# Two more chunks of a shared value quarter held in the lower half of a PSUM bank, with one bank for the weighted sums meanwhile

## The chip, the cores and the metric

The kernel runs on one core of a Trainium2 chip, in one launch. The metric is the time of the execution on the device in microseconds (us). Lower is better.

## What is computed

Eight batch rows, one token each, go through two identical layers. A layer is an attention step over a cache, added to its input, and then a small MLP mixer, added again. Both layers read the same weights and the same caches.

```python
B, Sq, D = 8, 1, 448
Hq, Hkv, Sk, Dh = 16, 8, 4096, 256
...
q = (x @ wq).reshape(B, Sq, Hq, Dh)            # transposed to B, Hq, Sq, Dh
scores = einsum("bhqd,bhkd->bhqk", q, k) * (Dh ** -0.5)
p = softmax(scores)
o = einsum("bhqk,bhkd->bhqd", p, v)            # back to B, Sq, Hq * Dh
return o @ wo
...
x = x + A(layernorm(x)); x = x + mixer_mlp(layernorm(x))     # layer 0
x = x + A(layernorm(x)); x = x + mixer_mlp(layernorm(x))     # layer 1
```

For each row and each of the 8 key-value heads there are 2 MB of keys and 2 MB of values (4096 x 256, bf16). Everything is needed once for layer 0 and, since the queries of layer 1 depend on the result of layer 0, once more for layer 1.

## The kernel before, in words

**Tiles and slots.** A head's 2 MB lie as 128 partitions x 32 positions x 256 values. They are loaded in quarters: a quarter is 8 chunks of 256 values on every partition, 4 KB per partition, 512 KB in all. SBUF has 30 slots for quarters (`QUARTERS`). A load of several neighbouring quarters can go out as one DMA; `next_kv` in the planner chooses slot and size, and `issue_kv` (L653 is the line of the DMA itself) writes the instruction.

**What is kept between the layers.** Some quarters of a row stay in their slots from layer 0 to layer 1: the keys of heads 3 to 6, the first quarter of the keys of head 7, the values of head 7, and quarters 1 to 3 of the values of head 6 (`KEPT_K`, `KEPT_V`). Two further quarters of the keys of head 7 wait as transposes in the four transpose banks of PSUM, and one more in `kh` and in the upper halves of the two banks `psP`. The first quarter of the values of head 6 (`PART_V`) is not kept whole. A part of it, `PART` = 512 of the 2048 values per partition (two chunks), is copied by ScalarE (ACT) into columns 256 to 511 of bank `psR` (L1318), after the first quarter's weighted sum in layer 0. In layer 1 the load of that quarter leaves out these values (`skip`), and ACT copies them back into the slot (L1277) when the rest has landed.

**A head's two halves of work.** `front(layer, b, h)` transposes the keys on TensorE (PE; L1544 into `psT`), evacuates them on VectorE (DVE) and ACT (L1473, L1474), forms the scores (L1156, or L1438 by rows) and the exponentials (L1246). `back(layer, b, h)` loads the values, forms the weighted sums in one of the two banks `psP`, quarter by quarter, copies the bank out (L1332 to L1338), turns it on PE into the same bank (L1345), reduces it on DVE (L1349, L1352), and projects it with `wo` (L1373, or L1093 for the last heads of a layer). The weighted sum has a wide form (L1289, whole bank) and a narrow one (L1296, lower half) that is used while the upper halves of `psP` hold keys (`upper`). The bank alternates with the count of backs:

```python
par = g % 2
ps, bk = psP[par], f"P{par}"
```

**The crossing.** For a row, heads 0 to 2 and then 3 to 7 pass layer 0. The MLP of layer 0, the queries of layer 1 and layer 1 follow, which begins with heads 6 and 7. Between head 7 of layer 0 and head 6 of layer 1 stand the backs of heads 0, 1 and 2 of the next row, whose values are loaded one quarter at a time. I call the stretch from head 6 of layer 0 to head 6 of layer 1 a crossing; there are eight, one per row, the first around 114 to 148 us, the third around 377 to 405, the sixth around 764 to 790. In the last crossing there is no next row, and backs of layer 1 of the row before stand in its place. Most slots hold kept quarters in a crossing, so the loads pass through the few others.

**The order of the work.** All operations are listed with their dependencies and priorities, and `schedule` lays them out with planned durations, engine by engine. The result is a fixed order for each engine, with semaphores. DMAs are issued by SP in order; an issue waits until the last reader of its slot is done. Where PE would stand idle in the plan, the planner puts in matmuls on an identity (`filler`, L1753), to hold the planned load of PE above a mark, and only into a bank that no operation has open (`bank_ev`).

Of the kernel before, what the change touches and what calls it, by code (L numbers as in the profile page):

```python
# [53 lines left out]
YC = 0  # L54
ST = 504
STR = 244
PART = 512
Q1 = 176
ROWS = True
SHORT = 0.1  # L60
# [2 lines left out]


class Op:
    __slots__ = ("dma_n", "eng", "emit", "dur", "deps", "prio", "idx", "name", "lat", "sem", "val",
                 "pos", "vc", "signal", "end", "nsucc", "succ", "raw", "dma", "tbank", "unit", "frees", "hot", "quiet")

    def __init__(self, eng, emit, dur, name, prio):
# [25 lines left out]
class Plan:  # L95
# [12 lines left out]
    def __init__(self):  # L108
        self.ops = []
        self.writer = {}  # L110
        self.readers = {}
        self.bank = {}
        self.filler = None
        self.issue_kv = None
        self.tenant = [None] * QUARTERS
        self.free_at = [0.0] * QUARTERS

    def op(self, eng, emit, dur, name, rd=(), wr=(), banks=(), prio=None, dma=None):
        o = Op(eng, emit, dur, name, len(self.ops) if prio is None else prio)
        o.idx = len(self.ops)  # L120
        o.dma = dma
        for k in rd:
            w = self.writer.get(k)
            if w is not None:
                o.deps[w] = True
        for k in wr:
            w = self.writer.get(k)
            if w is not None and w not in o.deps:
                o.deps[w] = False
            for r in self.readers.get(k, ()):  # L130
                if r is not o and r not in o.deps:
                    o.deps[r] = False
        for b in banks:
            for e, a in self.bank.get(b, {}).items():
                if a is not o and a not in o.deps:
                    o.deps[a] = False
        for k in rd:
            self.readers.setdefault(k, []).append(o)
        for k in wr:
            self.writer[k] = o  # L140
            self.readers[k] = []
        for b in banks:
            d = self.bank.setdefault(b, {})
            if eng == "pe":
                d["pe"] = o
            else:
                d[eng] = o
        self.ops.append(o)
        return o
# [15 lines left out]
    def schedule(self):  # L165
# [78 lines left out]
        while n < len(self.ops):  # L244
# [99 lines left out]
            quiet = quiet or o.quiet  # L344
            if o.tbank is not None:
                for x in o.tbank if isinstance(o.tbank, list) else [o.tbank]:
                    bank_ev[x] = True if e == "pe" else o
            o.pos = len(order[e])
            order[e].append(o)
            n += 1  # L350
# [131 lines left out]
def bass_interleave_layers__gqa_block_cached__mixer_s_mlp__decode_kernel(  # L482
# [125 lines left out]
    def slot_ap(x, a, n):  # L608

        return kv[:, x.slot * 2048 + a:x.slot * 2048 + a + n]  # L610
# [645 lines left out]
    def back(layer, b, h):  # L1256
# [5 lines left out]
        g = backs[0]  # L1262
        backs[0] += 1
        no = g % NO
        par = g % 2
        ps, bk = psP[par], f"P{par}"
        wide_pv = not upper[0]
        hi = len(plan.ops) - 10 ** 5
# [1 line left out]
        most = MOST if (layer == 0 and b and h in free_heads) else MOST2 if h == l2_heads[1] and layer else 4  # L1270
        if (layer, b, h) == (1, B - 1, free_heads[-1]):
            most = 1
        part = h == PART_V and layer
        assert not part or fresh_v == [0]
        vs.update(load(A_v_cache, b, h, fresh_v, keep_v, most, PART if part else 0))
        if part:
            plan.op("act", lambda a: a.copy(slot_ap(vs[0], 0, PART).bitcast(f32), psR[:, 2 * P:2 * P + PART // 2]), 0.4,  # L1277
                    "part", rd=["part", ("s", vs[0], 0)], wr=[("s", vs[0], 2)], banks=["R"], prio=hi)
        first = 4 * CH + len(plan.ops) if layer == 0 and b and h in free_heads else None
        turned = (layer, b) == (1, B - 1) and h in TURNED  # L1280
        for u in range(4):

            def pv(t, u=u, q=vs[u]):
                last = None
                for g in range(4 if wide_pv else 0):
                    k = 8 * g + 4 * (u // 2) + 2 * (u % 2) if in_rows else 8 * u + 2 * g
                    v = (slot_ap(q, 0, 2048).rearrange("p (a s x) -> p a s x", a=2, s=4)[:, :, g, :] if in_rows else
                         slot_ap(q, 512 * g, 512))
                    last = t.matmul(ps[32 * g:32 * g + 4, :], pT[nr][:, k:k + 2, :].rearrange("p k j -> p (k j)"),  # L1289
                                    v, start=(u == 0), stop=(u == 3), skip_group_check=True,  # L1290
                                    tile_position=(0, 32 * g))
                for s in range(0 if wide_pv else 8):
                    i = 8 * u + s
                    g4 = 32 * (i % 4)
                    k = 8 * (s % 4) + 4 * (u // 2) + 2 * (u % 2) + s // 4 if in_rows else i
                    last = t.matmul(ps[g4:g4 + 2, PV0:PV0 + DH], pT[nr][:, k, :],  # L1296
                                    slot_ap(q, s * 256, 256), start=(i < 4), stop=(i >= 28),
                                    skip_group_check=True, tile_position=(0, g4))
                return last

            def pv_turned(t, u=u, q=vs[u]):
                last = None
                for s in range(8):
                    k = 8 * (s % 4) + 4 * (u // 2) + 2 * (u % 2) + s // 4
                    for c in range(2):
                        last = t.matmul(ps[:, PV1 + 2 * c:PV1 + 2 * c + 2], slot_ap(q, s * 256, 256)[:, c:DH:2],
                                        pT[nr][:, k, :], start=(u == 0 and s == 0), stop=(u == 3 and s == 7),
                                        skip_group_check=True)
                return last
            fn, d = (pv_turned, (0.45, 0.47, 320, 16)) if turned else (pv, (0.25, 0.46, 512, 4 if wide_pv else 8))  # L1310
            o = plan.op("pe", fn, d, "pv",
                    rd=[("pT", nr, 0), ("pT", nr, 1), ("s", vs[u], 0), ("s", vs[u], 1),
                        "pz"] + [("s", vs[u], 2)] * bool(part and u == 0) + [("acc", 1) if u > 1 else ("o2", 1 - par)] * ((layer, b, h) == (1, B - 1, free_heads[-1]) and u > 0),
                    wr=[("pv", par, x) for x in range(u, 4)], banks=[bk], prio=first)
            if u == 0:
                o.tbank = bk
            if h == PART_V and not layer and u == 0:
                o = plan.op("act", lambda a: a.copy(psR[:, 2 * P:2 * P + PART // 2],  # L1318
                                                    slot_ap(vs[0], 0, PART).bitcast(f32)), 0.4, "part",
                            rd=[("s", vs[0], 0), ("pv", par, 0)], wr=["part"], banks=["R"], prio=hi)  # L1320
            if u not in keep_v:
                o.frees = [vs[u]]

# [94 lines left out]
    tcount = [0]  # L1418
    held_banks = set()
    upper = [False]  # L1420
    by_rows = {}

    def next_bank():
# [63 lines left out]
    def half_piece(x, pc):  # L1487

        if pc == 0:
            bank = tcount[0] % NT
            while tcount[0] % NT in held_banks:
                tcount[0] += 1
            bank = tcount[0] % NT
            tcount[0] += 1

            def tr(t):
                last = None
                for s in range(4):  # L1500
                    last = t.transpose(psT[bank][:, s * P:(s + 1) * P],
                                       slot_ap(x, s * 256, 256).bitcast(f32), ident_f[:, :])
                return last
            plan.op("pe", tr, (0.44, 0.86, 1024, 4), "tr", rd=[("s", x, 0), "ident_f"],
                    wr=[("psT", bank)], banks=[("T", bank)]).tbank = bank

            def ev(e):
                if e is nc.vector:
                    return e.tensor_copy(kh[:, :].bitcast(f32), psT[bank][:, :])
                return e.copy(kh[:, :].bitcast(f32), psT[bank][:, :])  # L1510
            plan.op("ev", ev, {"dve": 0.71, "act": 0.6}, "ev", rd=[("psT", bank)], wr=["kh", ("khb", 0), ("khb", 1)],
                    banks=[("T", bank)]).tbank = bank
            return
        upper[0] = True
        for i in range(2):
            def tr(t, i=i):
                last = None
                for s in range(2):
                    last = t.transpose(psP[i][:, DH + s * P:DH + (s + 1) * P],
                                       slot_ap(x, (4 + 2 * i + s) * 256, 256).bitcast(f32), ident_f[:, :])  # L1520
                return last
            plan.op("pe", tr, (0.25, 0.45, 512, 2), "tr", rd=[("s", x, 1), "ident_f"],
                    wr=[("ph", i)], banks=[f"P{i}"]).tbank = f"P{i}"
        for i in range(2):
            evac_half(i, lambda i=i: slot_ap(x, (4 + 2 * i) * 256, 512).bitcast(f32), ("s", x, 1, i))
# [287 lines left out]
```

## Time and profile before

| | |
|---|---|
| median of 3 runs | 1071.9 us (1071.61 to 1074.43) |
| profiled execution | 1069.21 us |
| its span, first to last instruction | 1067.4 us |
| PE busy | 944.8 us (89%) |
| DVE busy | 600.4 us (56%) |
| ACT busy | 337.4 us (32%) |
| main DMA queue | 432.79 MB, 98.6% of 16 engines' span |
| mean granted PE clock | 0.975 |
| copies into `psR` (L1318) | 8, median 0.376 us |
| copies out of `psR` (L1277) | 8, median 0.358 us |

Durations come from the one profiled execution, and the times from separate runs. Busy times are a union over an engine's instructions. The granted clock is the share of full speed that TensorE's throttle let through. The share of the DMA engines is the time that their packets took; it can come out slightly above 1 in a short stretch, since a packet is counted where it starts.

### The profile page before, as it was taken

What the parts mean: (1) busy time and instruction counts of PE and PEld (TensorE: products, weight loads), DVE (VectorE), ACT (ScalarE), POOL (GpSimd) and SP (SyncE); (2) the same over time, 40 slices, a digit from 0 to 9 for tenths busy, and PEclk for the clock granted to TensorE, in tenths of its full rate; (3) what the DMA queues carried; (4) which work ended last, traced back from release to release, by engine and by line L of the source; (5) the groups of instructions that cost most, each with busy time, mean ns of one, the idle gap of its engine ahead of it and who ended that gap; (6) DMA issues with size and microseconds to landing.
All of it is one profiled execution on the core that took longest, in us unless ns stands there. A gap on an engine that the chain in (4) does not pass through costs nothing.

```text
span 1067.4 us, 31572 instructions
## 1 busy us (share of the span) xinstructions
PE 944.8 (89%) x13891; PEld 655.5 (61%) x13891; DVE 600.4 (56%) x1951; ACT 337.4 (32%) x941; POOL 99.9 (9%) x284
## 2 busy tenths in 40 slices
PE   4989898898989889898898989988899899998896
PEld 3556665666656665566565666666666676566664
DVE  4445456555566546555465555655456565666464
ACT  1134122342233413354032531334214342253041
POOL 0000010010110001001010100101001000111011
PEclk9899999899999999999999999999989999999997
DMA  9999999999999999999999999999999999999995
GB/s 359 408 427 424 408 401 426 422 425 397 410 427 426 402 401 420 424 427 410 393 419 428 422 403 399 425 426 425 398 375 425 426 420 394 405 424 418 374 420 242
DMA packets 57236, 435.17 MB, mean 408 GB/s; under 512 B 6142, under 2 KB 9356, under 8 KB 34572
## 3 DMA queue, kind: packets, MB, share of 16 engines
q1 hardware_dynamic: 56932, 432.79, 98.6%
q8 instruction: 109, 1.79, 0.7%
q10 hardware_dynamic: 168, 0.38, 0.1%
q14 instruction: 27, 0.22, 0.1%
HBM read 433.14 MB, written 0.01 MB: 406 GB/s over the span
## 4 chain that ended last, share of the span: by engine, by line
DMA 50%; PE 40%; DVE 5%; SPq 2%; issue 1%; ACT 1%; POOL 0%
DMA kv<-in_A_v_cache_dram 25%; DMA kv<-in_A_k_cache_dram 24%; PE psT L1544 14%; PE psT L1438 5%; PE psP L1289 4%; PE psM L1156 3%; PE psP L1345 2%; PE psP L1296 2%; PE psR L1373 2%; PE psM L908 2%; SPq L635 1%; DVE kv L1473 1%; PE psM L1072 1%; DMA w_sb<-in_B_w_dram 1%; PE psP L1753 1%
## 5 line engine op out<-in xcount | busy, mean ns | idle before, releaser
L1544 PE MATMUL psT<-ident_f,kv 128*128 128x128 f32 x2752 | 375.2, 283 | 24.5 <-DMA kv<-in_A_k_cache_dram 21.2
L1544 PEld LDWEIGHTS psT<-ident_f,kv 128*128 128x128 f32 x2752 | 304.5, 143 | 100.6 <-issue 57.9
L1473 DVE COPY kv<-psT 128x512 f32<-128x512 f32 x388 | 266.1, 690 | 176.1 <-PE psT L1544 168.7
L1474 ACT COPY kv<-psT 128x512 f32<-128x512 f32 x332 | 193.6, 587 | 381.0 <-PE psT L1544 298.4
L1438 PE MATMUL psT<-kv,qz 128*32 128x512 bf16 x1664 | 131.3, 394 | 3.4 <-ACT kv L1474 2.4
L1236 POOL PARTITION_ALL_REDUCE gm<-pm x128 | 45.5, 356 | 763.8 <-DVE pm L1234 674.8
L1289 PE MATMUL psP<-kv,pT 128*4 128x512 bf16 x1376 | 105.5, 378 | 4.4 <-DMA kv<-in_A_v_cache_dram 3.7
L1246 ACT ACTIVATE pT<-sS,nb,fac 128x32 bf16<-128x32 bf16 x128 | 52.6, 417 | 124.9 <-DVE nb L1240 124.6
L1345 PE MATMUL psP<-ident_f,oS 128*128 128x128 f32 x252 | 61.7, 327 | 25.3 <-DVE oS L1334 16.4
L1373 PE MATMUL psR<-wo_sb,oT 128*1 128x192 bf16 (+1 forms) x888 | 66.4, 259 | 14.2 <-DVE oT L1352 11.5
L1345 PEld LDWEIGHTS psP<-ident_f,oS 128*128 128x128 f32 x252 | 39.9, 206 | 50.7 <-DVE oS L1334 34.1
L1250 POOL PARTITION_ALL_REDUCE Db<-rs x128 | 51.2, 400 | 185.7 <-ACT pT L1246 185.7
L1296 PE MATMUL psP<-kv,pT 128*2 128x256 bf16 x1280 | 59.0, 277 | 9.7 <-DMA kv<-in_A_v_cache_dram 8.8
L1438 PEld LDWEIGHTS psT<-kv,qz 128*32 128x32 bf16 x1664 | 32.8, 95 | 46.4 <-issue 13.0
L1246 ACT ACTIVATE pT<-sS,nb 128x32 bf16<-128x32 bf16 x128 | 40.7, 326 | 56.2 <-DVE nb L1240 56.2
L1373 PEld LDWEIGHTS psR<-wo_sb,oT 128*1 128x1 bf16 x888 | 36.7, 82 | 32.4 <-DVE oT L1352 18.3
L1332 DVE TENSOR_SCALAR oS<-psP,half_rows 128x256 f32<-128x256 f32 x86 | 41.3, 481 | 25.7 <-PE psP L1289 25.1
L1453 DVE CAST sr<-psT 128x512 bf16<-128x512 f32 x57 | 39.4, 691 | 28.3 <-PE psT L1438 28.1
L1289 PEld LDWEIGHTS psP<-kv,pT 128*4 128x4 bf16 x1376 | 30.9, 82 | 34.3 <-issue 8.6
L1156 PE MATMUL psM<-qz,kv 128*128 128x48 bf16 x1344 | 45.7, 184 | 5.6 <-DVE sS L1229 1.8
L1156 PEld LDWEIGHTS psM<-qz,kv 128*128 128x128 bf16 x1344 | 39.7, 97 | 14.5 <-issue 5.6
L1229 DVE CAST sS<-psM 128x64 bf16<-128x64 f32 x128 | 27.9, 218 | 32.9 <-PE psM L1156 24.5
(201 smaller groups left out, 922.3 us busy)
## 6 DMA issues: line engine op xcount, KB each, us to landing
kv<-in_A_k_cache_dram SPq DMA_DIRECT2D x68, 2048.0 KB, 22.7
kv<-in_A_v_cache_dram SPq DMA_DIRECT2D x59, 2048.0 KB, 17.2
kv<-in_A_v_cache_dram SPq DMA_DIRECT2D x155, 512.0 KB, 9.6
kv<-in_A_v_cache_dram SPq DMA_DIRECT2D x21, 1024.0 KB, 9.2
kv<-in_A_k_cache_dram SPq DMA_DIRECT2D x30, 512.0 KB, 9.1
kv<-in_A_k_cache_dram SPq DMA_DIRECT2D x10, 1536.0 KB, 18.3
kv<-in_A_k_cache_dram SPq DMA_DIRECT2D x10, 1024.0 KB, 8.8
kv<-in_A_v_cache_dram SPq DMA_DIRECT2D x5, 1536.0 KB, 9.2
```

The lines of the kernel that those rows point to most:

```text
L1156: last = t.matmul(ps[:, SB + 2 * i:SB + 2 * i + 2 * REP], a()[:, c:256:2], bcast(rhs(c), REP, 1), start=(c == 0), stop=(c == 1))
L1236: plan.op("pool", lambda gp: gp.partition_all_reduce(gm[nm][:, :], pm[nm][:, :], P, RO.max), 0.46, "max", rd=[("pm", nm)], wr=[("gm", nm)] ...
L1246: return a.activation(pT[nr][:, :, :].rearrange("p i j -> p j i")[:, jj, :], sview[:, jj, :], ACT.Exp, bias=nb[nm][:, jj:jj + 1], scale=sc ...
L1250: plan.op("pool", lambda gp: gp.partition_all_reduce(Db[nr][:, :], rs[nr][:, :], P, RO.add), 0.5, "sum", rd=[("rs", nr, 0), ("rs", nr, 1)] ...
L1289: last = t.matmul(ps[32 * g:32 * g + 4, :], pT[nr][:, k:k + 2, :].rearrange("p k j -> p (k j)"), v, start=(u == 0), stop=(u == 3), skip_gr ...
L1296: last = t.matmul(ps[g4:g4 + 2, PV0:PV0 + DH], pT[nr][:, k, :], slot_ap(q, s * 256, 256), start=(i < 4), stop=(i >= 28), skip_group_check= ...
L1345: last = t.transpose(ps[:, P * c:P * c + P], oS[:, c:DH:2], ident_f[:, :])
L1373: last = t.matmul(psR[r:r + 1, 0:w], oT[no][:, i % 2, i // 2:i // 2 + 1], wo_sb[:, a:a + w], start=(k == 1 and i == 0), stop=(k == turn_at ...
L1438: last = t.matmul(psT[bank][32 * g:32 * g + 32, :], qz[:, a:a + 32], slot_ap(qs[g // 2], g % 2 * 1024, 1024)[:, c:1024:2], start=(half == ...
L1473: return e.tensor_copy(dst, psT[bank][:, :])
L1474: return e.copy(dst, psT[bank][:, :])
L1544: last = t.transpose(psT[bank][:, s * P:(s + 1) * P], src, ident_f[:, :])
```

## The change

`PART` grows from 512 to 1024 values per partition. Four of the eight chunks of the first value quarter of head 6 are now held between the layers, two in `psR` as before and two in the lower half of `psP[1]`. The layer 1 load of the quarter is 256 KB in place of 384 KB. There are two copies in and two copies out in each crossing. While `psP[1]` is lent (from the front of head 7 in layer 0 to the back of head 6 in layer 1), the weighted sums go to `psP[0]` alone; elsewhere the banks alternate by the last one used. The planner regards the lent bank as closed to its identity matmuls from the copy in until the bank is used again.

```diff
-PART = 512
+PART = 1024
...
-                    bank_ev[x] = True if e == "pe" else o
+                    bank_ev[x] = True if e == "pe" or (o.lent and x == "P1") else o
...
-        par = g % 2
+        part = PART_V == h
+        if plan.lent and not (part and layer):
+            par = 0
+        else:
+            par = 1 if plan.lent else 1 - last_par[0]
+        last_par[0] = par
...
-        part = h == PART_V and layer
-        assert not part or fresh_v == [0]
-        vs.update(load(A_v_cache, b, h, fresh_v, keep_v, most, PART if part else 0))
-        if part:
-            plan.op("act", lambda a: a.copy(slot_ap(vs[0], 0, PART).bitcast(f32), psR[:, 2 * P:2 * P + PART // 2]), 0.4,
-                    "part", rd=["part", ("s", vs[0], 0)], wr=[("s", vs[0], 2)], banks=["R"], prio=hi)
+        restore = part and layer
+        assert not restore or fresh_v == [0]
+        vs.update(load(A_v_cache, b, h, fresh_v, keep_v, most, PART if restore else 0))
+        lends = [(psR, 2 * P, "R"), (psP[1], 0, "P1")]
+        if restore:
+            plan.lent = False
+            for i, (bank, at, key) in enumerate(lends):
+                o = plan.op("act", lambda a, i=i, bank=bank, at=at: a.copy(
+                    slot_ap(vs[0], 512 * i, 512).bitcast(f32), bank[:, at:at + 256]), 0.4, "part",
+                    rd=[("part", i), ("s", vs[0], 0)], wr=[("s", vs[0], 2 + i)], banks=[key], prio=hi)
+                if i:
+                    o.tbank = key
...
-            if h == PART_V and not layer and u == 0:
-                o = plan.op("act", lambda a: a.copy(psR[:, 2 * P:2 * P + PART // 2],
-                                                    slot_ap(vs[0], 0, PART).bitcast(f32)), 0.4, "part",
-                            rd=[("s", vs[0], 0), ("pv", par, 0)], wr=["part"], banks=["R"], prio=hi)
+            if part and not layer and u == 0:
+                for i, (bank, at, key) in enumerate(lends):
+                    o = plan.op("act", lambda a, i=i, bank=bank, at=at: a.copy(
+                        bank[:, at:at + 256], slot_ap(vs[0], 512 * i, 512).bitcast(f32)), 0.4, "part",
+                        rd=[("s", vs[0], 0), ("pv", par, 0)], wr=[("part", i)], banks=[key], prio=hi)
...
-        upper[0] = True
+        upper[0] = plan.lent = True
```

More of the change, by code (lines that the diff above doesn't have):

```diff
@@ L65 @@
 class Op:
-    __slots__ = ("dma_n", "eng", "emit", "dur", "deps", "prio", "idx", "name", "lat", "sem", "val",
+    __slots__ = ("dma_n", "lent", "eng", "emit", "dur", "deps", "prio", "idx", "name", "lat", "sem", "val",
                  "pos", "vc", "signal", "end", "nsucc", "succ", "raw", "dma", "tbank", "unit", "frees", "hot", "quiet")
@@ L116, in __init__ @@
         self.free_at = [0.0] * QUARTERS
+        self.lent = False
     def op(self, eng, emit, dur, name, rd=(), wr=(), banks=(), prio=None, dma=None):
@@ L121, in op @@
         o.dma = dma
+        o.lent = self.lent
         for k in rd:
@@ L1312, in back @@
                     rd=[("pT", nr, 0), ("pT", nr, 1), ("s", vs[u], 0), ("s", vs[u], 1),
-                        "pz"] + [("s", vs[u], 2)] * bool(part and u == 0) + [("acc", 1) if u > 1 else ("o2", 1 - par)] * ((layer, b, h) == (1, B - 1, free_heads[-1]) and u > 0),
+                        "pz"] + [("s", vs[0], 2), ("s", vs[0], 3)] * bool(restore and u == 0) + [("acc", 1) if u > 1 else ("o2", 1 - par)] * ((layer, b, h) == (1, B - 1, free_heads[-1]) and u > 0),
                     wr=[("pv", par, x) for x in range(u, 4)], banks=[bk], prio=first)
@@ L1420, in bass_interleave_layers__gqa_block_cached__mixer_s_mlp__decode_kernel @@
     upper = [False]
+    last_par = [1]
     by_rows = {}
```

## The prediction, made before the result was known

> **What bounds the kernel now.** The page first: the DMA row, the rate row, the queue table and the shares of the chain that ended last.
>
> ```profile
> span 1067.4 us, 31572 instructions
> ...
> DMA  9999999999999999999999999999999999999995
> GB/s 359 408 427 424 408 401 426 422 425 397 410 427 426 402 401 420 424 427 410 393 419 428 422 403 399 425 426 425 398 375 425 426 420 394 405 424 418 374 420 242
> ...
> q1 hardware_dynamic: 56932, 432.79, 98.6%
> ...
> DMA 50%; PE 40%; DVE 5%; SPq 2%; issue 1%; ACT 1%; POOL 0%
> ```
>
> The 16 DMA engines are full from start to end; only the rate sags, from 425 to about 400 GB/s, once in some 130 us. These sags are the crossings from layer 0 of one row to its layer 1. So I asked for stretches: everything up to 1055 us, an undisturbed stretch, the third crossing and the sixth (columns: stretch and length; busy time of PE, PEld, DVE, ACT, POOL; granted clock, DMA share, GB/s).
>
> ```profile
> 0.00:1055.00 1055.00, 938.25 (x13688) 649.78 (x13689) 595.83 (x1928) 337.22 (x940) 98.26 (x278) 0.98 1.00 412
> 288.00:360.00 72.00, 63.81 (x731) 43.71 (x731) 43.81 (x122) 26.69 (x73) 7.55 (x20) 0.98 1.01 425
> 383.30:399.10 15.80, 14.23 (x358) 10.19 (x358) 7.46 (x45) 0.21 (x1) 0.00 (x0) 1.00 1.03 404
> 767.70:783.50 15.80, 14.34 (x321) 10.15 (x321) 7.20 (x45) 0.21 (x1) 0.00 (x0) 0.81 0.95 346
> ```
>
> Up to 1055 us the bound is bytes; the 12.4 us behind that are a tail of compute. In the sixth crossing the clock fell to 0.81 of full and the rate to 346 GB/s: there slots came free too slowly.
>
> Then the DMA issues by size, and one issue of the sixth crossing asked for alone.
>
> ```profile
> kv<-in_A_v_cache_dram SPq DMA_DIRECT2D x155, 512.0 KB, 9.6
> ...
> kv<-in_A_v_cache_dram SPq DMA_DIRECT2D x8, 384.0 KB, 6.6
> ```
> ```profile
> kv<-in_A_v_cache_dram SPq DMA_DIRECT2D x1, 384.0 KB, 5.0
> ```
>
> The eight loads of 384 KB are the ones the change cuts. 5.0 us, with the queue nearly drained, is the shortest time from issue to landing of any kv load; 6.6 us means some 1.6 us of work queued ahead. That surplus decides whether a slot freed late costs anything.
>
> Last, the timeline of the third crossing, where head 7 of layer 0 ends and the next row's head 0 begins.
>
> ```profile
> 383.35 1.04 PE L1296 MATMUL psP<-kv,pT 128*2 128x256 bf16 x32 [0.45 <-DMA kv<-in_A_v_cache_dram]
> 384.45 0.42 DVE L1338 COPY oS<-psP 128x256 f32<-128x256 f32 x1 [1.67 <-PE psP L1296]
> ...
> 384.63 0.39 PE L1296 MATMUL psP<-kv,pT 128*2 128x256 bf16 x8 [0.23 <-DMA kv<-in_A_v_cache_dram]
> ...
> 384.95 0.51 PE L1345 MATMUL psP<-ident_f,oS 128*128 128x128 f32 x2
> 385.07 0.33 SPq L653 DMA_DIRECT2D kv<-in_A_v_cache_dram  x1
> 385.49 0.17 DVE L1349 TENSOR_REDUCE o<-psP 128x4 f32<-128x16 f32 x1 [0.62 <-PE psP L1345]
> ```
>
> Head 0's first quarter (384.63) starts while head 7's bank is still being copied, turned and reduced, and SP refills its slot at 385.07. That overlap needs the second bank.
>
> **Part 1: 128 KB less in each of eight loads.** 8 x 131,072 B = 1.049 MB. The main queue moved 432.79 MB in 98.6% of 1067.4 us, which is 411 GB/s: 2.55 us. At 425 GB/s it is 2.47, at the crossing's 404 it is 2.60. The rows per partition shrink from 3,072 to 2,048 bytes, a packet size that no kv load has now. The trace's packets of 3,072 B took 0.139 us on average (median 0.121) and those of 1,792 B 0.080 (0.076). On the line between them a 2,048 B packet takes 0.092 (0.085), and 1,024 packets over 16 engines save 0.047 x 64 = 3.0 us (0.036 x 64 = 2.3). I take 2.55, since bytes at the queue's own rate lie between. The section DMA Optimizations of the Trainium skill's page Perfetto Trace Analysis says that small DMAs, under 2 KB, pay much overhead per transfer; the rows cut here end exactly at that size. By that rule part of the saving would go; the trace has 22.4 GB/s on one engine at 1,792 B against 24.4 at 4,096 B, so little of it.
>
> **Part 2: sixteen more ACT copies.** L1318 takes 0.376 us, L1277 0.358: 8 x 0.73 = 5.9 us on an engine that is busy for 337 of 1067 us. In layer 0 the slot of V's first quarter comes free one copy (0.38 us) later, and SP waits there. In the third crossing that issue stands in the chain as 378.05, with 11.75 us to landing, 6.7 above the shortest, so 0; uncovered it would be 8 x 0.38 = 3.0. In layer 1 the second restore delays the head's first quarter of PE work by up to 0.36 us, at most 2.9 in all; the first one ended at 403.19 and PE began that head at 404.89, so 0 as well. Queued behind it on ACT are the exponentials and evacuations of the next head, with the same gap.
>
> **Part 3: one bank for five weighted sums.** Before, the parity gives heads 6 and 7 of layer 0 and the next row's 0, 1, 2 the banks 0, 1, 0, 1, 0. The change moves only head 7 and head 1; layer 1's head 6 stays in bank 1. Three starts now follow a head in the same bank. For head 0 the first quarter must wait for the reduce: 385.49 + 0.17 instead of 384.63, 1.1 us with the semaphore, and up to 1.8 if PE takes the projection (385.92 to 386.40) first. Queued behind that matmul is all of PE's order, and SP behind the slot. SP's issue of 385.07 moves to about 386.5; it landed after 7.3 us, so 5.9 are left, above 5.0: hidden. In the sixth crossing the same issue (768.97, 6.8 us) is left with 5.0 to 5.7: just hidden. Head 1 started at 391.48, after the reduce at 391.16: 0. Head 2's start moves by 0.2 to 0.4 us. I charge 0.3 us in all, for the sixth and eighth crossings. The floor is 0, since a later start frees nothing earlier; uncovered in all eight it is 8 x 1.1 = 8.8.
>
> **Part 4: the plan is laid anew.** Every order of the five engines comes from planned times, so 0.3 us less per crossing shuffles what follows. The crossings were all planned by one code and still differ from 404 to 346 GB/s, so this term has either sign. Taken as 0, with 1.5 us to each side.
>
> **Sum.** -2.55 + 0 + 0 + 0.3 = -2.25 us. The profiled execution took 1069.2 us (span 1067.4 and 1.8 around it) and would take 1067.0, of which span 1065.1. The median of the three runs is 2.7 above it; taken from that median, 1071.9, the result is 1069.6.
>
> **Rival, slower: the clock.** The planner pads idle PE time with matmuls on an identity (L1753), into a bank that no sum is using. In the crossing the four transpose banks hold K of head 7, so the two psP banks are all there is, and afterwards none while a sum is open. The padding in heads 0 to 2 of the crossings one, three, five and six:
>
> ```profile
> 126.00:141.20 15.20, 2.90 (x12) 1.50 (x12) 0.89 1.03 398
> ...
> 384.60:401.20 16.60, 0.56 (x2) 0.20 (x2) 1.00 1.02 402
> ...
> 640.30:656.60 16.30, 1.25 (x5) 0.41 (x5) 1.00 1.02 392
> 769.90:787.60 17.70, 1.19 (x5) 0.42 (x5) 0.81 0.95 336
> ```
>
> One cold crossing costs (404 - 346) x 15.8 / 404 = 2.3 us up to 783.5, and 0.9 in the next 7 us at 350 GB/s: 3.2 together. It turns the sign from 5.5 us on (3.2 over no change, and 2.3 saved), so from two more crossings like it: -2.3 + 6.4 = +4.1, **1076.0**. For: most of this padding has to go. Against: it is 1 to 12 matmuls in 15 us, three crossings stayed at 1.00 with one or two, and the sixth went cold with five. The section A second HAM failure mode: psum-queue depth-cycling of the Trainium skill's page TensorE: Matmul & The Clock Gate speaks against the change: micro-idling between matmul groups that cycle through PSUM banks makes the clock flip between half and full. By that rule fewer banks in rotation mean more pauses and more such stretches; the trace shows the flip (0.81), but not that banks caused it. Chance 0.20.
>
> **Rival, faster: a slow crossing is repaired.** The new order may fill the sixth crossing better: its 2.9 us (336 against 402 GB/s over 17.7 us) come on top, -5.2, **1066.7**. For: nothing in its work differs from the third's. Against: only two or three crossings have anything to repair. Chance 0.24.
>
> **Rival, nothing: the load is hidden.** If SP waits for the scores of layer 1 (in the third crossing the next K issue came 4.1 us after the one before), a shorter V load only lengthens that wait: +0.3, **1072.2**. Against: that K load still took 6.8 us, so 1.8 were queued and the engines never paused. Chance 0.06.
>
> **How the numbers follow.** 0.3% of 1071.9 is 3.2 us, about what a measurement of this kernel can tell from no change. The forecast case has 0.50; its terms (2.3 to 3.0 saved, 1.5 of replanning) put 0.17 of that beyond -3.2. Faster: 0.17 + 0.24 = 0.41. Same: 0.33 + 0.06 = 0.39. Slower: 0.20. The forecast case alone reaches from 1067.5 to 1071.5. The range takes in the repaired crossing and two cold ones, 1066.0 to 1077.0, and leaves out about 0.1 on each side, such as three cold crossings or two repaired ones.
>
> **What would show it.** Right: eight V loads of 256 KB, HBM read lower by 1.05 MB, sixteen copies on each of the two new lines, the rate in the crossings near 400 GB/s, clock about 0.975 over the span, and head 0's first quarter behind the reduce. Wrong: more stretches below 0.9 of the clock between 110 and 1015 us, issues of 512 KB that land after 5.0 us in most crossings, or a DMA share below 0.97 there.

## The result: slower by 0.86%, and outside the forecast's range

The changed kernel takes 1080.23 us (median of 6 runs, 1077.12 to 1083.12). The kernel before, run beside it, takes 1071.76 (1067.13 to 1074.43). The ratio is 1.0086 with a 95% interval of 1.0056 to 1.0115. (The ratios here and below are the recorded ones; they can differ by 0.1 to 0.2% from the quotient of two medians.) The forecast was 1069.6, in a range that ended at 1077.0.

The page of the changed kernel, by the same rows as before (its profiled execution took 1078.67 us). PEclk is added: the granted clock in tenths, slice by slice.

```profile
span 1076.9 us, 31523 instructions
...
PEclk9999799999999989999999997999989999999897
...
GB/s 353 408 427 423 410 392 425 424 422 369 393 425 426 419 394 417 425 427 417 381 425 425 426 408 363 425 425 424 406 349 427 425 418 373 402 425 417 332 422 230
...
q1 hardware_dynamic: 55924, 431.74, 98.0%
...
DMA 46%; PE 44%; DVE 6%; issue 1%; ACT 1%; SPq 1%; POOL 0%
...
kv<-in_A_v_cache_dram SPq DMA_DIRECT2D x8, 256.0 KB, 6.5
```

The bytes are down by the 1.05 MB forecast (432.79 to 431.74), and the eight cut loads are there. The undisturbed slices still run at 425 GB/s. What is worse is the sags: 332 to 394 GB/s in the slowest slice of each crossing, where it had been 374 to 401. The chain has moved four points from DMA to PE. The queue's idle time, which is the span times the share not used, went from 14.9 us (1.4% of 1067.4) to 21.5 (2.0% of 1076.9).

To put a number on the sags I took, from the trace, the stretch of each crossing from 5 us before the first copy into `psR` to 15 us after the first copy out of it, and subtracted from its length what its bytes take at 425 GB/s. Over the eight crossings this loss was 22.5 us before and is 34.7 now. The 12.2 us more, less the 2.5 us that the missing bytes save, make 9.7, and the span is longer by 9.5.

The fifth crossing shows how a head now starts. First the kernel before: its timeline, then its DMA from 640 to 654 us (an issue row ends with the count, the KB of each and the median us to landing), then the row of that stretch, with granted clock, DMA share and GB/s at its end.

```profile
645.23 0.42 DVE L1338 COPY oS<-psP 128x256 f32<-128x256 f32 x1
645.42 0.39 PE L1296 MATMUL psP<-kv,pT 128*2 128x256 bf16 x8 [0.16 <-DMA kv<-in_A_v_cache_dram]
```
```profile
DMA packets 1533, 5.49 MB, mean 392 GB/s; under 512 B 170, under 2 KB 170, under 8 KB 1531
...
kv<-in_A_v_cache_dram SPq DMA_DIRECT2D x9, 512.0 KB, 6.8
...
640.00:654.00 14.00, 13.41 (x330) 9.75 (x331) 6.71 (x44) 0.21 (x1) 0.00 (x0) 1.00 1.02 392
```

The next head's first quarter starts 0.19 us after the copy out begins, as soon as its data is there (the wait shown is for the DMA). That is the earliest of three such starts in this crossing; the other two came 0.91 and 1.03 us after their copies began. A 512 KB load takes 6.8 us, 1.8 above the 5.0 of the shortest in this trace: there is work queued. Now the changed kernel, the same crossing: timeline, and DMA and clock from 642 to 656.6 us.

```profile
641.93 0.42 DVE L1352 COPY oS<-psP 128x256 f32<-128x256 f32 x1 [2.58 <-PE psP L1309]
...
643.14 0.18 DVE L1363 TENSOR_REDUCE o<-psP 128x4 f32<-128x16 f32 x1 [0.80 <-PE psP L1359]
...
643.47 1.02 PE L1309 MATMUL psP<-kv,pT 128*2 128x256 bf16 x16 [0.36 <-DVE o L1363]
...
648.01 0.42 DVE L1352 COPY oS<-psP 128x256 f32<-128x256 f32 x1
...
649.22 0.17 DVE L1363 TENSOR_REDUCE o<-psP 128x4 f32<-128x16 f32 x1
...
649.54 1.02 PE L1309 MATMUL psP<-kv,pT 128*2 128x256 bf16 x16 [0.36 <-DVE o L1363]
...
653.19 0.42 DVE L1352 COPY oS<-psP 128x256 f32<-128x256 f32 x1 [3.51 <-PE psP L1309]
...
```
```profile
DMA packets 1476, 5.15 MB, mean 353 GB/s; under 512 B 164, under 2 KB 164, under 8 KB 1474
...
kv<-in_A_v_cache_dram SPq DMA_DIRECT2D x9, 512.0 KB, 5.7
...
642.00:656.60 14.60, 13.33 (x259) 8.45 (x260) 6.55 (x42) 0.21 (x1) 0.00 (x0) 0.51 0.98 353
```

Copy out, turn and reduce now stand between one head's sum and the next, and the releaser of the next sum is the reduce (`DVE o L1363`). From the copy's start to the next sum it takes 1.54 us at 641.93, and 1.53 again at 648.01. By then two quarters are waiting: the group has 16 matmuls, so the first slot comes free late and the second close behind it (SP issues at 644.11 and 644.53). The loads land after 5.7 us instead of 6.8, and the rate is 353 GB/s. Loads that land near 5.0 us are the sign the prediction had named for being wrong. That figure is no floor, though: four loads of 512 KB in the changed kernel landed after 4.5 to 4.8 us. And this crossing cannot tell the late starts from the clock, since it ran at a granted clock of 0.51, against 1.00 before.

The second crossing is the cleaner view, because both kernels have the full clock (1.00) in the 12 us from the start of head 7's sum. Before, then after:

```profile
256.05 0.42 DVE L1338 COPY oS<-psP 128x256 f32<-128x256 f32 x1 [1.51 <-PE psP L1296]
256.24 0.39 PE L1296 MATMUL psP<-kv,pT 128*2 128x256 bf16 x8 [0.24 <-DMA kv<-in_A_v_cache_dram]
...
256.67 2.28 SPq L653 DMA_DIRECT2D kv<-in_A_v_cache_dram  x2
```
```profile
258.33 0.42 DVE L1352 COPY oS<-psP 128x256 f32<-128x256 f32 x1 [1.95 <-PE psP L1309]
...
259.35 0.17 DVE L1363 TENSOR_REDUCE o<-psP 128x4 f32<-128x16 f32 x1 [0.60 <-PE psP L1359]
...
259.68 0.61 PE L1309 MATMUL psP<-kv,pT 128*2 128x256 bf16 x16 [0.36 <-DVE o L1363]
260.11 2.37 SPq L655 DMA_DIRECT2D kv<-in_A_v_cache_dram  x3
```

The next sum starts 1.35 us after the copy begins, where it had been 0.19, and SP's first issue comes 1.78 us after it, where it had been 0.62. In those 12 us (from 254.9 before, from 257.2 after) the rate is 344 GB/s against 382. Yet the loads issued in them land after 7.1 us in the median, against 6.7 before. So a load that takes long to land does not show that nothing was lost. One crossing is no proof by itself: the two-bank kernel of the next section has one of 358 GB/s at full clock too, its third.

Over all 32 such boundaries between narrow sums, the mean time from the copy's start to the next sum rose from 1.76 us to 2.55; 8 had been under 0.6 us and none is now. Loads of K and V that land in under 6.0 us (issued after 100 us) went from 10 to 28. The view of the waits has a row of the changed kernel that the kernel before does not have:

```profile
PE psP L1309 <- DVE o L1363: 4.7, 13, 0.4
```

### The profile page after: what moved, and what is told of

It is laid out like the page before. It is cut to its first block, busy times and chain, and to the rows that moved or that the text cites. A ratio compares the mean times of both kernels' runs of the same rounds, so it can differ in the third digit from the quotient of the medians.

```text
span 1076.9 us, 31523 instructions
## 1 busy us (share of the span) xinstructions
PE 947.9 (88%) x13856; PEld 657.8 (61%) x13856; DVE 590.7 (55%) x1933; ACT 352.9 (33%) x975; POOL 99.9 (9%) x284
## 3 DMA queue, kind: packets, MB, share of 16 engines
q1 hardware_dynamic: 55924, 431.74, 98.0%
## 4 chain that ended last, share of the span: by engine, by line
DMA 46%; PE 44%; DVE 6%; issue 1%; ACT 1%; SPq 1%; POOL 0%
DMA kv<-in_A_v_cache_dram 24%; DMA kv<-in_A_k_cache_dram 22%; PE psT L1559 15%; PE psT L1453 6%; PE psP L1302 5%; PE psP L1309 3%; PE psP L1359 3%; PE psM L1158 3%; PE psR L1387 2%; PE psM L910 2%; PE psM L1074 1%; PE psP L1768 1%; DVE oS L1346 1%; DVE kv L1488 1%; DVE oS L1348 1%
## 5 line engine op out<-in xcount | busy, mean ns | idle before, releaser
L1488 DVE COPY kv<-psT 128x512 f32<-128x512 f32 x369 | 254.0, 691 | 171.2 <-PE psT L1559 163.9
L1489 ACT COPY kv<-psT 128x512 f32<-128x512 f32 x351 | 204.7, 587 | 377.1 <-PE psT L1559 296.6
L1359 PE MATMUL psP<-ident_f,oS 128*128 128x128 f32 x252 | 62.9, 333 | 33.9 <-DVE oS L1348 19.5
L1387 PE MATMUL psR<-wo_sb,oT 128*1 128x192 bf16 (+1 forms) x888 | 69.8, 270 | 15.0 <-DVE oT L1366 12.5
L1309 PE MATMUL psP<-kv,pT 128*2 128x256 bf16 x1280 | 62.8, 301 | 13.6 <-DMA kv<-in_A_v_cache_dram 8.1
L1387 PEld LDWEIGHTS psR<-wo_sb,oT 128*1 128x1 bf16 x888 | 39.0, 84 | 32.8 <-DVE oT L1366 18.4
```

Source lines behind the costliest of these rows:

```text
L1359: last = t.transpose(ps[:, P * c:P * c + P], oS[:, c:DH:2], ident_f[:, :])
L1387: last = t.matmul(psR[r:r + 1, 0:w], oT[no][:, i % 2, i // 2:i // 2 + 1], wo_sb[:, a:a + w], start=(k == 1 and i == 0), stop=(k == turn_at ...
L1488: return e.tensor_copy(dst, psT[bank][:, :])
L1489: return e.copy(dst, psT[bank][:, :])
```

## The experiments

Every ratio is to the kernel before, run on the same chip in the same set; brackets are 95% intervals. For a difference of two ratios I give the half-width as the root of the sum of squares of theirs. Nearly all kernels have their orders laid anew by the planner, so a single pair also carries what that does. Losses in the crossings, half-clock time (the part of those stretches with a granted clock of 0.5) and times from copy to sum come from the one profiled execution of each kernel.

### The saving alone, one bank alone, the padding alone

My theory after the result: the price is the one bank, because PE starts each next head later and the slots come free later. The rival was the forecast's own, the clock: less room for padding.

**Two banks, short loads.** The loan goes nowhere but `psR`, where the second pair of chunks takes the place of the first. The banks alternate, and the padding has its room again.

```diff
-        lends = [(psR, 2 * P, "R"), (psP[1], 0, "P1")]
+        lends = [(psR, 2 * P, "R"), (psR, 2 * P, "R")]
...
+        par = 1 - last_par[0]
```

> The changed kernel with two banks for the weighted sums throughout and nothing lent: the second pair of chunks is copied into the same columns of psR as the first and restored from there (so these two chunks take wrong values; loads of 256 KB, all 32 copies and the padding as before). If the loss comes from giving up the second bank, by either way below (idle PE and clock, or late first quarters), this is the saving without its price: 1069.5 us (1067 to 1072), clock about 0.975. If it comes from the copies on ACT or from the short load, it stays at 1078 to 1082. If it is chance in the replanned order, anything between.

Measured: 1065.27 us, 0.9962 [0.9945, 0.9978]. It lies below the expected range, in a set in which the kernel before was 3 us faster too. The saving is real, and the 32 copies cost nothing that shows. The change itself, 1.0086, stands 1.24% +- 0.34 above it: that is what the one bank, with the loan in it and the padding's lost room, costs there, some 13 us.

**One bank, old loads.** The change with `PART` of before; `psP[1]` stays empty in the crossing and closed to the padding.

```diff
-PART = 1024
+PART = 512
-        lends = [(psR, 2 * P, "R"), (psP[1], 0, "P1")]
+        lends = [(psR, 2 * P, "R")]
```

> The changed kernel with PART = 512, so no chunk goes into psP[1] and the load is 384 KB again, but the sums of the crossing stay in psP[0] alone and psP[1] stays closed to the identity matmuls. Either theory of the lost bank: the changed kernel plus the saving it gave up, 1082.5 us (1079 to 1086). If copies or short load are to blame: 1072, as before the change.

Measured: 1075.79 us, 1.0061 [1.0037, 1.0085]. That is below the expected range. A saving of 0.38% and a price of 0.61% would put the change at 0.23% +- 0.29, but it stands at 0.86% +- 0.30. The other 0.63% +- 0.42 is not explained by these parts: with one bank the short load may save less, or the loan in `psP[1]` may cost something, and no run here separates the two.

**The same with room for the padding.** `psP[1]` is open to the identity matmuls.

```diff
-                    bank_ev[x] = True if e == "pe" or (o.lent and x == "P1") else o
+                    bank_ev[x] = True if e == "pe" else o
```

> As e2, but the free lower half of psP[1] is open to identity matmuls all through the crossing, so PE can be padded even while a sum is open. Theory clock (the missing identity matmuls let PE go cold): back to 1072 us (1070 to 1074), cold stretches in crossings gone. Theory late quarters (a head's first quarter waits for the reduce of the head before, so slots are refilled late): no help, 1079 to 1085 us, at a clock of 0.97 or more.

Measured: 1078.91 us, 1.0086 [1.0055, 1.0117]. Its row of clock, against 0.952 in the changed kernel:

```profile
core 0: 1080.3 us, clock 0.973
```

The clock is back, the time is not.

**The kernel before with the padding's room cut.** Two banks, and the padding may go only where the change leaves it room.

```diff
-                    b = [(x.end if x else -1.0, k) for k, x in bank_ev.items() if x is not True]
+                    b = [(x.end if x else -1.0, k) for k, x in bank_ev.items() if x is not True and not (lent and (
+                        k == "P1" or (k == "P0" and bank_ev.get("P1") is True)))]
```

> The kernel before the change, sums alternating between two banks, but while the upper halves are in use the planner may put identity matmuls into psP[0] alone and only when neither bank has a sum open, which is the room that the change leaves. Theory clock: 1078 to 1082 us, with cold stretches in most crossings, clock near 0.955. Theory late quarters: 1072 us (1070 to 1074).

Measured: 1070.18 us, 1.0015 [0.9991, 1.0039]. With two banks, the room for padding is worth at most 0.39%. Its crossings spent 37.5 us at half clock, against 64.9 in the changed kernel, so it does not show what a clock as low as there would cost. These four say: with the old loads the one bank costs 6.5 us +- 2.6 and 9.2 us +- 3.3, and a mean clock of 0.973 does not take that away.

### Is it the hold, the ring of slots, or both?

**Turn and reduce aside.** One bank for the sums, old loads, room for padding, but the turn and the reduce go into the empty lower half of `psP[1]`: `psP[0]` is free as soon as it is copied out. (Shown in part; the reduce reads from `tp` too.)

```diff
+            tp, tk = (psP[1], "P1") if aside else (ps, bk)
-                    last = t.transpose(ps[:, P * c:P * c + P], ...)
+                    last = t.transpose(tp[:, P * c:P * c + P], ...)
```

> As e3 (PART = 512, sums of the crossing in psP[0] alone), but the turn and the reduce that follow a sum go into the free lower half of psP[1], so psP[0] is free for the next head after the copy out, about 0.9 us earlier per head. Theory late quarters: most of the price comes back, 1072 us (1070 to 1075) where the kernel before is at 1070, and fewer loads that land within 6 us of their issue than in e3. If the price has another origin than how long a head holds the bank, it stays at 1077 to 1081.

Measured: 1070.57 us, 1.0012 [0.9995, 1.0029]. Against the kernel that differs only in that (1.0086) it is 0.74% +- 0.35 better. Copy to next sum is back at 1.73 us, and 8 of 32 are under 0.6.

**One slot more for the ring.** If the ring is what makes a late start dear, a seventh slot should buy the cover back. A quarter less of V is kept (`KEEP_V` 6, no chunks of V held in PSUM), with two banks and with one.

```diff
-KEEP_V = 7
+KEEP_V = 6
-    PART_V = HKV - 1 - KEEP_V // 4
+    PART_V = -1
```

> The kernel before with one value quarter less kept between the layers (KEEP_V = 6) and no chunks held in PSUM: 640 KB more per row to load (5.2 MB, 12.8 us at 411 GB/s), but seven slots instead of six for the loads of the crossing. Two banks. 1082 us (1079 to 1085) where the kernel before is at 1070: it is the base for e7.

> As e6, but with the sums of the crossing in psP[0] alone. Theory late quarters: with seven slots a slot may be 1.27 us later before the loads run dry, so the one bank costs at most 3 us over e6 (it cost 7 to 10 with six slots). If the price of the one bank doesn't depend on how far the loads run ahead: 7 to 10 us over e6.

Measured: 1078.24 us, 1.0093 [1.0070, 1.0115] with two banks; 1082.45, 1.0134 [1.0107, 1.0160] with one. One bank costs 0.41% +- 0.35 here, 4.4 us. Loads that land in under 6.0 us are 1 and 5. At most 3 us had been expected; 4.4 us is above that, but the interval takes it in. With six slots and the same room for padding one bank cost 0.86% +- 0.31, so the difference is 0.45% +- 0.47: how much of the price the ring explains stays open.

**The change once more**, beside these three.

> The changed kernel again, beside the others on one chip: ratio 1.0086 to the kernel before, 1077 to 1080 us.

Measured: 1077.93 us, 1.0096 [1.0064, 1.0128]; loss in the crossings 35.2 us (34.7 in the first profile).

### A correct version that frees the bank early

If the hold is the price, a turn that needs no bank of the sums should let the loan stand. Instead of transposing, two matmuls with a selector of zeros and ones put the four columns of `oT` into a few columns of another bank.

```diff
+                def pick(t):
+                    for c in range(2):
+                        last = t.matmul(psM[:, 60 + 2 * c:62 + 2 * c], oS[:, c:DH:2], self_f[:, :], ...)
```

**Into `psM`**, with the change, and as a control with old loads and two banks:

> The changed kernel in full (four chunks held, one bank in the crossing), but a sum taken in the crossing is not turned in its own bank: after the copy out two matmuls of the copy with a 0/1 selector write the four wanted columns into a spare corner of psM, and DVE scales them from there. So psP[0] is free after the copy out, as in e5. Theory late quarters: the saving of e1 (4 us) less the remnant that e5 showed (1 to 3 us): 1067 us where the kernel before is at 1069 (1065 to 1070), faster than both. If the second loan in psP[1] costs something of its own, 1073 or more.

> A control for e9: the selector matmuls into psM in the kernel with two banks and two chunks (PART = 512), for all sums taken while the upper halves are in use. Theory late quarters: the bank was not short there, so no gain over the kernel before: 1069 us (1067 to 1071).

Measured: 1102.83 us, 1.0301 [1.0273, 1.0329], and 1090.81, 1.0160 [1.0121, 1.0198]. A clear miss. The control loses too, and it has two banks, so the selector matmuls in `psM` have a price of their own. The scores and the MLP use that bank; that this is why is argued, and the next kernel bears on it.

**Into the last four columns of `psP[1]`'s lower half**, whose 16 bytes per partition of lent values go to a small SBUF tile; then the same with more padding, some of it into the open sum with zero weights.

```diff
+        lends = [(rest, 0, 4, 1016, []), (psR, 2 * P, 256, 0, ["R"]), (psP[1], 0, 252, 512, ["P1"])]
```

> The changed kernel with the selector matmuls of e9, but into the last four columns of the lower half of psP[1], a bank that no other work of the crossing uses; the last 16 bytes per partition of the lent chunks wait in SBUF instead (a third small copy each way). psP[0] is free after the copy out. Theory late quarters, with e9's price explained by sharing psM with scores and MLP: the saving of e1 (4 us) less the remnant of e5 (1 to 2): 1067.5 us where the kernel before is at 1069.5 (1066 to 1070). If the selector matmuls themselves are the price of e9 and e10: 1085 or more, as there.

> e11 with more padding of PE in the crossing: the planner's mark for planned PE load is raised from 3500 to 5500 columns per window while psP[1] is lent, and while a sum is open in psP[0] it may add matmuls with sixteen zero columns as weights, which add 0 to the open sum (60 of these, and 77 more identity matmuls). If what e11 lost against e5 (0.6%) is PE at half clock for 96 us of its crossings, this takes a good part back: 1066 to 1071 us where the kernel before is at 1069, with under 40 us cold in the crossings. If the loans in psP[1] themselves (copies, waits for the bank) are its price, 1075 to 1080, whatever the clock.

Measured: 1076.89 us, 1.0074 [1.0049, 1.0099], and 1075.95, 1.0073 [1.0054, 1.0093]. Moving the selector matmuls out of `psM` took 2.27% +- 0.38 off (1.0301 to 1.0074). Between the kernel with the corner and the padded one, half-clock time in the crossings fell from 96 us to 27, and the time stayed. The early bank (copy to next sum 1.65 and 1.74 us) did not bring back what it had brought with the turn aside. So two more kernels took the parts of this one singly.

### Selector matmuls, loan, short loads and padding, one at a time

**Selector matmuls with old loads**, and **turn aside with short loads**, both with nothing lent in `psP[1]`.

```diff
-        lends = [(rest, 0, 4, 1016, []), (psR, 2 * P, 256, 0, ["R"]), (psP[1], 0, 252, 512, ["P1"])]
+        lends = [(psR, 2 * P, 256, 0, ["R"])]
```
```diff
-        lends = [(psR, 2 * P, "R")]
+        lends = [(psR, 2 * P, "R"), (psR, 2 * P, "R")]
```

> The loads of the kernel before (512 KB, one pair of chunks lent, nothing in the second bank), one bank for the narrow sums, and after each sum the selector matmuls of the kernel with the corner, into the last four columns of the second bank's lower half, in place of the turn; the padding is kept off the second bank. If the selector matmuls are the price that the kernel with the corner kept: +0.7 to +1.1 per cent over the kernel before, which is 1077 to 1081 us where that takes 1069. If the loan itself is the price: within 0.2 per cent of the kernel before, about 1070 us.

> The loads of the change (256 KB, thirty-two copies out and in), one bank for the narrow sums, turn and reduce in the second bank, where nothing is lent: the second pair of chunks goes into the same columns as the first, so two chunks of a quarter take wrong values. The saving of the short load with two banks was 0.38 per cent, and one bank that is free after the copy out cost 0.12 per cent: if the two add, 0.26 per cent under the kernel before, 1066 us where that takes 1069, whether the selector matmuls or the loan cost the kernel with the corner its time. If a short load and one bank cost something together that neither costs alone: 1075 us or more.

Measured: 1082.14 us, 1.0121 [1.0079, 1.0163], and 1071.29, 1.0002 [0.9981, 1.0023]. The loan is not needed for the loss. The first is 0.47% +- 0.49 above its twin with loan and short loads, about the saving, though not clear of nothing. The second is no better than the kernel before, where 0.26% less was expected. The two are 0.28% +- 0.32 apart, so whether the parts add up is not settled.

The first differed from the kernel with the turn aside in the padding too, which was kept off `psP[1]`. **Selector matmuls with the room** (the edit shown), and **turn aside without it** (the old line kept):

```diff
-                    bank_ev[x] = True if e == "pe" or (o.lent and x == "P1") else o
+                    bank_ev[x] = True if e == "pe" else o
```

> The kernel with selector matmuls and nothing lent, but the padding may use the second bank between them, as it may in the kernel with the turn aside. If the selector matmuls are the price: +0.9 to +1.4 per cent, 1079 to 1085 us where the kernel before takes 1070. If the missing room for padding is: within 0.3 per cent of the kernel before, 1067 to 1073 us.

> The kernel with turn and reduce in the second bank, but the padding is kept off that bank, as in the kernel with selector matmuls. If the selector matmuls are the price: +0.1 to +0.3 per cent, 1070 to 1073 us where the kernel before takes 1070, as with the room. If the missing room for padding is: +0.9 to +1.4 per cent, 1079 to 1085 us.

Measured: 1077.00 us, 1.0069 [1.0043, 1.0095], and 1074.86, 1.0041 [1.0014, 1.0068]. Neither theory alone: both came out in between.

Four kernels with the old loads and one bank for the sums now make a square:

| above the kernel before, % | padding kept off `psP[1]` | padding allowed there |
|---|---|---|
| turn and reduce in the sums' bank | 0.61 +- 0.24 | 0.86 +- 0.31 |
| turn and reduce in `psP[1]` | 0.41 +- 0.27 | 0.12 +- 0.17 |

Freeing the bank early is worth 0.74 +- 0.35 with the room and 0.20 +- 0.36 without it. The room is worth 0.29 +- 0.32 when the bank is free early and less than nothing (-0.25 +- 0.39) when it is held. Only the kernel with both back is level with the kernel before. The loss in the crossings of the profiled executions is 32.6 and 33.6 us above, 33.9 and 22.8 below, against 22.5 before: again only the lower right is level. But three of these four profiles, all except the lower right, caught the longest run of their kernel, so these losses may be too large for their medians. The lower left one was profiled at 1081.18 us, at the top of its ten runs (1070.26 to 1081.18), with half a clock for 78 us of its crossings, against 10 us in the one beside it.

**What follows.** That one bank for the sums, with the loan and the padding's room that go with it, is the price of the change is shown: the change (1.0086) and its twin with two banks (0.9962) are 1.24% +- 0.34 apart. That the hold through turn and reduce is a part of it is shown with the room there. That it is all of it is not: with the room gone, freeing the bank gives back little that can be measured. A reading that fits the square is that a slot comes free at the later of two delays, the hold and a slow PE, so that taking one away uncovers the other; that is argued, not tested. The selector matmuls cost 0.57% +- 0.31 more than the turn, with the room (1.0069 against 1.0012), and 0.80% +- 0.50 without it (1.0121 against 1.0041); why was not tried.

The clock may still be a part. The runs of one and the same kernel, with the same orders, were longer where the mean granted clock was lower, in all but one of the seventeen kernels. In the ten runs of the turn aside without the room (1070.26 us at 0.961, 1081.18 at 0.944; correlation -0.89) and the nine of the selector matmuls with it (-0.91), 0.01 of the clock went with about 5 us. Whether the clock made these runs longer, or longer waits lowered the clock, this does not tell.

No version with the right values beat the kernel before.

## Why the prediction was wrong, by its steps

**Part 1 (-2.55 us): right.** 1.05 MB fewer, and with two banks the time fell by 0.38% +- 0.17, which is 4.1 us +- 1.8 of 1068.61; 2.55 lies inside. In the changed kernel's trace a packet of 2,048 B took 0.092 us on average (median 0.084), as the line in the prediction had it. The section DMA Optimizations of the Trainium skill's page Perfetto Trace Analysis warns of much overhead per transfer in DMAs under 2 KB. At exactly that size the packets here moved 22.3 GB/s on one engine, against 23.8 at 4,096 B in the same trace and 22.1 at 3,072 B before, so little of it shows.

**Part 2 (0): right.** The two-bank kernel has all 32 copies and is faster.

**Part 3 (+0.3 us): this is the step that failed.** With the old loads one bank measured 0.61% and 0.86%, 6.5 and 9.2 us, and in the change itself 1.24%, some 13 us. The start behind the reduce was right: 1.1 to 1.8 us later had been worked out, and in the second crossing it came 1.35 us after the copy's start in place of 0.19. So was the time left for the load: in the third crossing the issue behind that start landed after 6.0 us, where the prediction had 5.9. The error was what it concluded from that: "so 5.9 are left, above 5.0: hidden". That was worked out for the third crossing and the sixth, and the third had lost least of the eight (1.8 us). In the second crossing the same issue (260.11) landed after 5.9 us, and the rate still was 344 GB/s against 382, at full clock in both kernels. Time to landing above the shortest one seen was no proof of cover, and 5.0 us was not the shortest possible either (4.5 in the changed kernel).

Two more things were left out. The delay does not come once in a crossing: in the fifth, head 0, head 1 and head 2 start 1.54, 1.53 and 2.33 us after the copy before them. And head 1's start "after the reduce at 391.16: 0" was read from the old order; in the new order the row `PE psP L1309 <- DVE o L1363` has 13 waits. The waits in that row come to only 4.7 us, since PE has other work in the meantime; that the price is paid by the slots and not by PE is read from the late issues, not tested. Since 8 x 1.1 = 8.8 counts one late start in each crossing, it was no upper bound, and that it lies between 6.5 and 9.2 is in part chance.

**Part 4 (0 +- 1.5 us): not settled.** Some pairs, such as the room given to the held bank (-0.25% +- 0.39), could be replanning or nothing.

**Rival, slower (1076.0, 0.20): the side was right, the mechanism is not the whole.** Half-clock time in the crossings rose from 16.6 us to 64.9 and the mean clock fell to 0.952. But the kernel with its clock back at 0.973 stayed at +0.86%, the one with two banks and the padding cut lost 0.15% +- 0.24, and the corner kernel with 68 us less of half clock did not move. The section A second HAM failure mode: psum-queue depth-cycling of the Trainium skill's page TensorE: Matmul & The Clock Gate tells of a clock that goes back and forth between half and full because PE idles briefly between groups of matmuls that cycle through PSUM banks. The trace agrees that the clock flips (64.9 us of half clock against 16.6). That fewer banks mean more flips is not on that page; it was the prediction's own step. The kernel with the clock back shows that the flips were not needed for the loss. Only with the bank freed early may the room count, 0.29% +- 0.32.

**The other rivals.** No slow crossing was repaired, and the load was not hidden, since the two-bank kernel kept its saving. Of the named signs of error two came true: more stretches below 0.9, and 512 KB loads that land near 5.0 us (within 5.3 us in five of the eight crossings).

## What to carry to other kernels

When a change removes the second buffer of a chain, price the whole hold of the one that stays (here copy, turn and reduce) at every place where it recurs, and charge it uncovered unless the cover is shown to hold at each of them. Read the cover from the worst stretch, not from the best one, and from the rate, not from the time to landing alone. A resource that was spare may serve two purposes (here a bank for overlap and for padding), and giving back one of them alone may give back little.

## What was not expected of the hardware

At half clock a quarter of a narrow sum (8 matmuls) took 0.60 us against 0.39, and the copy that precedes it took 0.42 in both: the hold from the copy's start to the reduce's end stretched from 1.2 us (258.33 to 259.52) to 1.4 only (641.93 to 643.32), while that part of PE's work grew by half. The turn-aside kernel also varied more from run to run without the room for padding: over 10.9 us in ten runs, against 4.5 with it (1068.08 to 1072.59).
